# A scale block in two column halves, and a weight fold in three bursts, in a fused attention and feed-forward kernel

## The chip, the cores and the metric

The kernel runs on one core of a Trainium2 chip. The metric is the device time of one execution in microseconds (us). Engines go by the profile's short names: PE is TensorE's matmuls and PEld its weight loads, DVE is VectorE, ACT is ScalarE, POOL is GpSimd, SP is SyncE, which issues most DMAs.

## What is computed

A transformer block with adaptive layer norm. A conditioning vector `c` gives six modulation rows of 1024 (shift, scale and gate for each half of the block). The first half is a linear attention with 32 heads of 32, the second a SwiGLU feed-forward of width 3584. The sequence has 2048 rows.

```python
mod = (_silu(c) @ w_mod).reshape(c.shape[0], 6, 1, -1)
sa, ca, ga, sb, cb, gb = ...
h = _layernorm(x, axis=-1) * (1 + ca) + sa
x = x + ga * _A_ref(h, A_wqkv, A_wo)
h = _layernorm(x, axis=-1) * (1 + cb) + sb
x = x + gb * _B_ref(h, B_w_gate, B_w_up, B_w_down)
...
# _A_ref: qkv of x @ wqkv, phi(t) = where(t > 0, t + 1, exp(t)) + 1e-6
kv = jnp.einsum('bhsd,bhse->bhde', pk, v)
z = jnp.einsum('bhsd->bhd', pk)
num = jnp.einsum('bhqd,bhde->bhqe', pq, kv)
den = jnp.einsum('bhqd,bhd->bhq', pq, z)[..., None] + 1e-06
o = num / den
```

## The kernel before

The 2048 rows are worked in four super-tiles of 512 rows (`sc`), each of four row tiles of 128 (`t`). The 1024 columns of the model are eight blocks of 128 (`cc`, or `j` for the rows of `w_mod`). Weights and large activations live in a pool of 19 buffers of 8 KB per partition (`k8`, by `big`); input tiles and their normalised forms in `k2`; PSUM has two pools of four banks, `pa` (`acc_a`) and `pb` (`acc_b`). All matmuls go through `mm` (line 98), which keeps them on TensorE in the order of the program text, and transposes through `transpose` (line 101). In the opening, the block under `in_order` fixes the order of VectorE, ScalarE and GpSimd too. Elsewhere those engines are ordered by the compiler's scheduler, and `tc.issue_after` ties one instruction behind another on its engine.

The opening (lines 124 to 145 and 465 to 529) does this. SP loads two tiles of x, then the scale block of `w_mod` (`wca`, eight loads of 256 KB), then the value weights `wv` (eight loads) with two more x tiles among them, the shift block `wsa` (eight) and the key weights `wk` (eight). The conditioning vector is turned into a column tile `scT` with SiLU. Warming matmuls (`keep_warm`, `keep_warm_f32`) fill TensorE. `mod_rows(1, ...)` multiplies `scT`, spread over 32 columns (`sc32`), with the rows of the whole scale block, as row products into `mod_ps`; the first column block is also made as a column (`first`). `mod_turn` turns the rows by VectorE into columns `ca0T`. Meanwhile x tiles are normalised (`ln1_stats`, `ln1_norm`), transposed by TensorE (`pe_transpose_tile`) into `hT`, and scaled by `scale_to` into `hs`. The shift isn't needed for values at this point (it is added later through `vb`). Then come the value products `v_mms`: groups of a row tile and a column half, `k_groups`. Four groups (row tiles 0 and 1) run side by side through all eight `cc`, then the groups of tile 2, then of tile 3, with the shift block's rows between. At the end `modulate_all` makes the modulated `hT` in place for the key products (`k_phase`), which follow.

`sc_row`, the SiLU of `c` on every partition, is made by eight matmuls and two ScalarE copies (lines 485 to 489). It is used by `mod_step` on VectorE (line 396), which makes later modulation rows.

After the opening the phases are key, (`kv_phase` of the super-tile before,) value, and so on; then the query products (`q_phase`). The key-value product is folded into the output weights: `fold_wo` (lines 602 to 611) multiplies 32x32 blocks of `KVT` with rows of `wo`, and writes the result over `wo`. It is called four times, between query groups. Each call fills four banks of `pb`: for each of four column groups `i`, the four row groups `g`, 16 products in all. `wo_tile` uses the folded weights, and the feed-forward (`gate_up`, `down`) takes the rest of the time.

Of the kernel before, what the change touches and what calls it, by code (L numbers as in the profile page):

```python
# [8 lines left out]
ACT = mybir.ActivationFunctionType  # L9
# [12 lines left out]
def kernel(  # L22
# [91 lines left out]
    c_sb = const.tile([DC, P], BF16, name="c_sb")  # L114

# [8 lines left out]
    for st in range(2):  # L124
        load_x(st, nc.sync)
# [3 lines left out]
    wca = [big("wme", [4, D]) for _ in range(2)]  # L129
# [6 lines left out]
    for j in range(DC):  # L136
        load_block(wca, wm_v, j, D, nc.scalar if j == 0 else nc.sync)
    for cc in range(DC):
        load_block(wv, wqkv_v, cc, 2 * D)
        if cc in (1, 4):  # L140
            load_x(2 + cc // 4, nc.sync)
# [26 lines left out]
    sc_row = const.tile([P, D], BF16, name="sc_row")  # L168
# [35 lines left out]
    def normalise(dst, src, mean, rstd):  # L204
        nc.vector.tensor_scalar(out=dst, in0=src, scalar1=mean, scalar2=rstd, op0=ALU.subtract, op1=ALU.mult)

    def normalise_act(dst, src, mv, rstd):
        nmr = small.tile([P, 1], F32, name="nmr")
        last_nmr[0] = nc.gpsimd.tensor_scalar(out=nmr[:], in0=mv[:, 0, 0:1], scalar1=rstd[:, 0:1], scalar2=-1.0,  # L209
                                op0=ALU.mult, op1=ALU.mult)  # L210
        nc.scalar.activation(out=dst, in_=src, func=ACT.Identity, bias=nmr[:], scale=rstd[:, 0:1])  # L211
# [20 lines left out]
    def ln1_norm(sc, t, x_sb, mv, rstd, dve=False):  # L232
        xn = k2.tile([P, D], BF16, name="xn", bufs=4)
        if dve:
            normalise(xn[:], x_sb[:], mv[:, 0, 0:1], rstd[:, 0:1])
        else:
            normalise_act(xn[:], x_sb[:], mv, rstd)
        if sc > 0:
            last_load[0] = nc.sync.dma_start_transpose(hTs[sc][:, :, t * P:(t + 1) * P], xn[:])
        return xn  # L240
# [14 lines left out]
    def mod_rows(q, lo, hi, first=None):  # L255
        for j in range(lo, hi):
            if first is not None:
                mm(first, lhsT=wca[j // 4][:, j % 4, 0:P], rhs=scT[:, j:j + 1], start=False, stop=j == DC - 1)
            row_matvec(mod_ps[:, q * MW:(q + 1) * MW], sc32[:, j, :], (wsa, wca)[q][j // 4][:, j % 4, :],
                       q == 0 and j == 0, j == DC - 1)  # L260
# [195 lines left out]
    def keep_warm(acc, n):  # L456
        for _ in range(n):
            mm(acc[:], lhsT=sel[:, 0, :], rhs=sel[:], start=True, stop=True)

# [8 lines left out]
    keep_warm(spare, 1)  # L468
# [5 lines left out]
    with in_order(nc.vector, nc.scalar, nc.gpsimd):  # L474
        mod_ps = acc_b("mod_ps")
        mm(mod_ps[:, 0:DC], lhsT=c_sb[:], rhs=ident[0:DC, 0:DC], start=True, stop=True)
        for g in range(4):
            mm(mod_ps[g * DH:(g + 1) * DH, MW:2 * MW], lhsT=ident[:, 0:DH], rhs=base_t[:, 0:MW], start=True, stop=False)
        nc.scalar.activation(out=scT[:], in_=mod_ps[:, 0:DC], func=ACT.Silu)
        xn0 = ln1_norm(*ln1_stats(0, 0))  # L480
        st1 = ln1_stats(0, 1)
        nc.vector.tensor_copy(out=sc32[:], in_=scT[:].unsqueeze(2).to_broadcast([P, DC, DH]))
        xn1 = ln1_norm(*st1, dve=True)
        keep_warm_f32(spare, 1)
        for h in range(2):
            for j in range(DC // 2):
                mm(accs[h][:, j * P:(j + 1) * P], lhsT=scT[:, 4 * h + j:4 * h + j + 1].to_broadcast([P, P]), rhs=ident[:],
                   start=True, stop=True)
            nc.scalar.copy(out=sc_row[:, h * NB:(h + 1) * NB], in_=accs[h][:])
        keep_warm(spare, 3)  # L490
        first = accs[2][:, 0:1]
        mm(first, lhsT=ident[:], rhs=base_t[:, 0:1], start=True, stop=False)
        mod_rows(1, 0, 3, first)
        pe_transpose_tile(hT, xn0, 0)
        pe_transpose_tile(hT, xn1, 1)
        mod_rows(1, 3, DC, first)
        keep_warm(spare, 1)
        nc.vector.tensor_scalar(out=hs[:, 0, 0:H], in0=hT[:, 0, 0:H], scalar1=first, scalar2=None, op0=ALU.mult)
        mod_turn(DC, 2 * DC)
        for cc in range(1, 4):  # L500
            scale_to(hs, hT, cc, 0, H)
        xn2 = ln1_norm(*ln1_stats(0, 2))
        for cc in range(4, DC):
            scale_to(hs, hT, cc, 0, H)
        st3 = ln1_stats(0, 3)
        gs = k_groups[0:4]
        v_mms(hs, gs, accs, 0, 6)
        pe_transpose_tile(hT, xn2, 2)
        for cc in range(DC):
            scale_to(hs, hT, cc, H, H + P)  # L510
        xn3 = ln1_norm(*st3)
        v_mms(hs, gs, accs, 6, DC)
        gs2, accs2 = k_groups[4:6], [acc_b("acc") for _ in range(2)]
        v_mms(hs, gs2[0:1], accs2[0:1])
        v_evac(0, gs, accs)
        pe_transpose_tile(hT, xn3, 3)
        for cc in range(DC):
            scale_to(hs, hT, cc, H + P, SCW)
        v_mms(hs, gs2[1:2], accs2[1:2])
        mod_rows(0, 0, DC)  # L520
        mod_turn(0, DC)
        nc.vector.tensor_copy(out=sca[:], in_=scr[:, :, :, 0])
        v_evac(0, gs2, accs2)
        for g in k_groups[6:8]:
            acc = acc_a()
            v_mms(hs, [g], [acc])
            v_evac(0, [g], [acc])
        modulate_all(hT, ca1T, saT)
        nc.vector.tensor_copy(out=sc32[:], in_=saT.unsqueeze(2).to_broadcast([P, DC, DH]))
# [11 lines left out]
    for sc in range(NSC):  # L541
        if sc > 0:
            k_phase(sc, 0, 2)
            kv_phase(sc - 1)
            k_phase(sc, 2, 3)
# [40 lines left out]
        if sc == 0:  # L586
            with tc.issue_after(last_load[0].ins):
                last_load[0] = mod_load(2, gaT)

    q_phase(1, 0, 1, 2)  # L590
    q_phase(1, 1, 2)
# [10 lines left out]
    def fold_wo(h, nb):  # L602
        ns = slice(nb * NB, (nb + 1) * NB)
        ps = [acc_b("wf") for _ in range(4)]
        for i in range(HPC):
            for g in range(4):
                rs = slice(g * DH, (g + 1) * DH)
                mm(ps[g][i * DH:(i + 1) * DH, :], lhsT=KVT[rs, h, i * DH:(i + 1) * DH], rhs=wo[h][rs, i, ns],
                   start=True, stop=True)
        for g in range(4):  # L610
            (nc.scalar.copy if g % 2 == 0 else nc.vector.tensor_copy)(out=wo[h][:, g, ns], in_=ps[g][:])

    q_phase(1, 2, 5)
# [5 lines left out]
    den_sum(0, acc_a())  # L619
    fold_wo(0, 0)  # L620
    den_spread(0)
    q_phase(1, 6, 8)
    fold_wo(0, 1)
    q_phase(2, 0, 2)
    fold_wo(1, 0)
    q_phase(2, 2, 4)
    fold_wo(1, 1)
# [3 lines left out]
    def wo_tile(st):  # L631
# [10 lines left out]
        for nb in range(NNB):  # L642
            ns = slice(nb * NB, (nb + 1) * NB)
            a_ps = acc_b("a_ps")
            for hg in range(HG):
                mm(a_ps[:], lhsT=pq[:, hg, t * P:(t + 1) * P], rhs=wo[hg // 4][:, hg % 4, ns],
                                 start=(hg == 0), stop=(hg == HG - 1))
# [144 lines left out]
```

## Time and profile before

| What | Value |
|---|---|
| Median of 6 runs | 829.98 us (829.82 to 831.26) |
| Profiled execution, time | 830.38 us |
| Profiled execution, span from first to last instruction | 828.6 us |
| First value product starts | 11.80 us |
| First key product starts | 27.78 us |
| Four bursts of the fold start | 155.32, 159.24, 163.16, 167.09 us |
| x_sb loads: issue to landing, median | 5.3 us |

Times within the execution count from its first instruction. A line of a timeline has the start, the length, the engine, the line of the kernel, the operation and its output and inputs; "x16" means that 16 like instructions were merged, and a bracket says how long the engine was idle before and what ended that. A line of the chain of waits has a start, a length, and what the chain was on. The length of a single matmul contains its passage through the array, so successive ones overlap: the difference of two starts is what one costs.

### The profile page before, as it was taken

The numbers are of one execution on the slowest core, as the hardware profiler recorded it, in microseconds if no ns is written. First come the engines' busy times: TensorE is split into PE (matmuls) and PEld (weight loads), VectorE is DVE, ScalarE is ACT, GpSimd is POOL, SyncE is SP. The second block draws the span as 40 slices with busy tenths as digits, with TensorE's granted clock in tenths as the row PEclk, the third lists the DMA queues.
The fourth block names the chain that finished last, engine by engine and source line by source line (L and its number), as shares of the span: only waits on it lengthen the run. The fifth ranks groups of instructions, "written<-read, shape, count | busy, mean of one in ns | idle before, by whom it ended". The sixth has DMA issues, their size and how long they took to land.

```text
span 828.6 us, 11287 instructions
## 1 busy us (share of the span) xinstructions
PE 823.0 (99%) x4609; PEld 379.0 (46%) x4609; DVE 348.7 (42%) x680; ACT 168.3 (20%) x253; POOL 64.1 (8%) x165
## 2 busy tenths in 40 slices
PE   8999999999999999999999999999999999999998
PEld 4444444444444444444444444444444444444444
DVE  6868778886353344422222354222224432222222
ACT  3535343434111101101111010111111101111000
POOL 2101020120222101000000010000001100000000
PEclk9999999999999999999999999999999999999999
DMA  9978454139996736446242272753405529610011
GB/s 343 305 167 187 115 120 102 36 101 317 368 231 213 246 115 190 138 162 212 93 157 97 61 221 90 254 188 108 146 0 181 149 66 357 218 46 1 19 58 51
DMA packets 142212, 129.07 MB, mean 156 GB/s; under 512 B 58768, under 2 KB 120720, under 8 KB 141648
## 3 DMA queue, kind: packets, MB, share of 16 engines
q1 hardware_dynamic: 138208, 115.10, 46.2%
q0 software_dynamic: 3792, 12.98, 5.2%
q8 instruction: 36, 0.59, 0.3%
q10 hardware_dynamic: 160, 0.26, 0.1%
q14 instruction: 16, 0.13, 0.1%
HBM read 101.98 MB, written 12.72 MB: 138 GB/s over the span
## 4 chain that ended last, share of the span: by engine, by line
PE 98%; DMA 1%; DVE 0%; ACTq 0%; issue 0%
PE acc L98 90%; PE a_ps L98 7%; DMA wme<-in_w_mod_dram 1%; PE kvp L98 1%; PE wf L98 0%; PE den L98 0%; PE mod_ps L98 0%; PE tp L101 0%; PE vb L98 0%; ACTq L126 0%; DVE e L708 0%; DVE ob L711 0%
## 5 line engine op out<-in xcount | busy, mean ns | idle before, releaser
L98 PE MATMUL acc<-h2T,wgu 128*128 128x512 bf16 x1792 | 387.6, 379 | 0.0
L98 PEld LDWEIGHTS <-wgu 128*128 128x128 bf16 x1792 | 175.3, 98 | 211.3
L687 DVE TENSOR_TENSOR gu<-acc,e 128x512 bf16<-128x512 f32 x112 | 77.4, 691 | 289.9 <-PE acc L98 287.1
L98 PE MATMUL acc<-wd,gu 128*128 128x512 bf16 (+2 forms) x924 | 196.1, 373 | 0.0
L686 ACT ACTIVATE e<-acc 128x512 f32<-128x512 f32 x112 | 67.0, 598 | 374.7 <-PE acc L98 374.7
L98 PEld LDWEIGHTS <-gu 128*128 128x128 bf16 x924 | 89.3, 98 | 104.5
L708 DVE TENSOR_TENSOR e<-acc,gb_bc 128x512 f32<-128x512 f32 (+2 forms) x33 | 22.3, 675 | 131.7 <-PE acc L98 128.8
L98 PEld LDWEIGHTS <-hT 128*128 128x128 bf16 x448 | 43.6, 98 | 52.3
L98 PE MATMUL a_ps<-wo,pq 128*128 128x512 bf16 x256 | 57.4, 379 | 0.0
L98 PE MATMUL acc<-hT,wq 128*128 128x512 bf16 x256 | 56.7, 379 | 0.0
L98 PE MATMUL acc<-wk,hT 128*128 128x512 bf16 x256 | 56.4, 379 | 0.0
L273 ACT ACTIVATE eb<-acc 128x512 bf16<-128x512 f32 x64 | 37.7, 594 | 62.0 <-PE acc L98 59.8
L211 ACT ACTIVATE xn<-x,nmr,rstd 128x1024 bf16<-128x1024 f32 x16 | 19.8, 1240 | 126.2 <-POOL nmr L209 126.2
L98 PE MATMUL acc<-wv,hT 128*128 128x512 bf16 x192 | 41.9, 379 | 0.0
L98 PEld LDWEIGHTS <-pq 128*128 128x128 bf16 x256 | 25.1, 98 | 30.2
L655 POOL DMA_DIRECT2D x_scratch<-x x16 | 9.8, 615 | 373.4 <-DVE x L648 373.3
L98 PEld LDWEIGHTS <-wq 128*128 128x128 bf16 x256 | 24.6, 98 | 29.9 <-issue 1.1
L274 DVE TENSOR_SCALAR eb<-eb 128x512 bf16<-128x512 bf16 x64 | 18.3, 290 | 26.3 <-ACT eb L273 26.3
L648 DVE TENSOR_TENSOR x<-a_ps,x_sb 128x512 f32<-128x512 f32 x32 | 22.1, 691 | 8.6 <-PE a_ps L98 8.6
L195 POOL TENSOR_TENSOR rstd<-veps,neg_half 128x1 f32<-128x1 f32 x32 | 18.0, 562 | 99.6 <-DVE veps L193 86.8
L711 DVE TENSOR_TENSOR ob<-e,x1r 128x512 bf16<-128x512 f32 (+2 forms) x33 | 22.3, 675 | 1.0
L201 DVE BATCH_NORM_STATS2 stats<-x_sb 128x6 f32<-128x512 bf16 x32 | 20.9, 674 | 4.0 <-DMA x_sb<-in_A_x_dram 3.9
(99 smaller groups left out, 320.9 us busy)
## 6 DMA issues: line engine op xcount, KB each, us to landing
wgu<-in_B_w_gate_dram SPq DMA_DIRECT2D x28, 1024.0 KB, 7.0
wgu<-in_B_w_up_dram SPq DMA_DIRECT2D x28, 1024.0 KB, 8.1
x_sb<-in_A_x_dram SPq DMA_DIRECT2D x32, 256.0 KB, 5.3
x_scratch<-x POOLq DMA_DIRECT2D x16, 512.0 KB, 3.1
x1r<-x_scratch SPq DMA_DIRECT2D x31, 256.0 KB, 2.8
wd<-in_B_w_down_dram SPq DMA_DIRECT2D x7, 1024.0 KB, 7.3
rbc<-rden_scratch POOLq DMA_DIRECT2D x16, 256.0 KB, 8.5
out_dram<-ob SPq DMA_DIRECT2D x31, 128.0 KB, 1.7
```

The lines of the kernel that those rows point to most:

```text
L98: return tc.keep_in_program_order(nc.tensor.matmul(out, lhsT=lhsT, rhs=rhs, start=start, stop=stop))
L195: nc.gpsimd.tensor_tensor(out=rstd[:, 0:n], in0=veps[:, 0:n], in1=neg_half[:].to_broadcast([P, n]), op=ALU.pow)
L201: nc.vector.bn_stats(out=stats[:, i, :], in_=src[:, i * NB:(i + 1) * NB])
L211: nc.scalar.activation(out=dst, in_=src, func=ACT.Identity, bias=nmr[:], scale=rstd[:, 0:1])
L273: nc.scalar.activation(out=e[:], in_=acc, func=ACT.Exp)
L274: nc.vector.tensor_scalar(out=e[:], in0=e[:], scalar1=1.0, scalar2=PHI_EPS, op0=ALU.min, op1=ALU.add)
L648: nc.vector.tensor_tensor(out=x1[:, ns], in0=a_ps[:], in1=x_t[:, ns], op=ALU.add)
L655: nc.gpsimd.dma_start(out=x1_dram[st * P:(st + 1) * P, :], in_=x1[:])
L686: nc.scalar.activation(out=sg[:], in_=ps[0][:], func=ACT.Silu)
L687: gm = nc.vector.tensor_tensor(out=guT[sc][f // GPT][:, f % GPT, :], in0=ps[1][:], in1=sg[:], op=ALU.mult)
L708: nc.vector.tensor_tensor(out=yt, in0=y_ps, in1=gb_bc[:, ns], op=ALU.mult)
L711: nc.vector.tensor_tensor(out=ob, in0=yt, in1=x1r, op=ALU.add)
```

## The change

The scale block is loaded as two halves of 512 columns. The first half is computed as columns, each of four column blocks by 16 matmuls of one column into PSUM (`ca_cols`), beside the transposes, which are written to two PSUM tiles by column half (`turn_half`). VectorE scales the first half of row tiles 0 and 1 straight from PSUM by the PSUM columns; ScalarE makes the unscaled copies. The value products of row tiles 0 and 1 run over `cc` 0 to 3, then the second half of the scale block is made as rows (`ca_rows`), then row tile 2 runs over `cc` 0 to 3, and then all over `cc` 4 to 7. The first two tiles are both normalised by ScalarE, in two pieces. `sc_row` is now loaded as one row, put through SiLU on ScalarE, written to DRAM and loaded back on all partitions. The rows of the shift block stand between the two groups of row tile 3, and the last modulation runs in two row halves. `kv_phase` moves one key group forward, and one query group forward at the end. The fold writes to new tiles `wof`, and its 16 units run in three bursts of 5, 6 and 5.

```diff
-    for st in range(2):
+    for st in range(3):
         load_x(st, nc.sync)
...
-    for j in range(DC):
-        load_block(wca, wm_v, j, D, nc.scalar if j == 0 else nc.sync)
-    for cc in range(DC):
-        load_block(wv, wqkv_v, cc, 2 * D)
-        if cc in (1, 4):
-            load_x(2 + cc // 4, nc.sync)
+    def load_ca(h, eng0):
+        for k in range(4):
+            js = slice(2 * k, 2 * k + 2)
+            (eng0 if k == 0 else nc.sync).dma_start(out=wca[h][:, js, :], in_=wm_v[:, js, D + h * NB:D + (h + 1) * NB])
+
+    load_ca(0, nc.scalar)
+    nc.scalar.dma_start(out=sc_row[0:1, :], in_=c)
+    for cc in range(4):
+        load_block(wv, wqkv_v, cc, 2 * D)
+    load_ca(1, nc.sync)
+    load_x(3, nc.sync)
+    for cc in range(4, DC):
+        load_block(wv, wqkv_v, cc, 2 * D)
...
-        xn0 = ln1_norm(*ln1_stats(0, 0))
-        st1 = ln1_stats(0, 1)
+        xn0 = ln1_norm(*ln1_stats(0, 0), 2)
+        xn1 = ln1_norm(*ln1_stats(0, 1), 2)
+        st2 = ln1_stats(0, 2)
+        col0 = acc_b("col0")
+        cols = [col0[:, 0:1]] + [mod_ps[:, DC + i:DC + i + 1] for i in range(3)]
+        tps = [acc_b("tp", (4, H), BF16) for _ in range(2)]
+
+        def turn_half(xn, t, h):
+            for i in range(4):
+                transpose(tps[h][:, i, t * P:(t + 1) * P], xn[:, (4 * h + i) * P:(4 * h + i + 1) * P])
+
+        def ca_cols(k):
+            for i in range(4):
+                for j in (2 * k, 2 * k + 1):
+                    mm(cols[i], lhsT=wca[0][:, j, i * P:(i + 1) * P], rhs=scT[:, j:j + 1], start=False,
+                       stop=j == DC - 1 and i in (0, 3))
+
+        mm(cols[0], lhsT=ident[:], rhs=base_t[:, 0:1], start=True, stop=False)
+        mm(mod_ps[:, DC:DC + 3], lhsT=ident[:], rhs=base_t[:, 0:3], start=True, stop=False)
+        keep_warm_f32(spare, 2)
+        ca_cols(0)
+        turn_half(xn0, 0, 0)
+        ca_cols(1)
+        turn_half(xn0, 0, 1)
+        ca_cols(2)
+        turn_half(xn1, 1, 0)
+        ca_cols(3)
+        for cc in range(4):
+            nc.vector.tensor_scalar(out=hs[:, cc, 0:H], in0=tps[0][:, cc, :], scalar1=cols[cc], scalar2=None, op0=ALU.mult)
+        nc.scalar.copy(out=ca0T[:, 0:1], in_=cols[0])
+        nc.scalar.copy(out=ca0T[:, 1:4], in_=mod_ps[:, DC:DC + 3])
+        nc.scalar.copy(out=hT[:, 0:4, 0:H], in_=tps[0][:])
         nc.vector.tensor_copy(out=sc32[:], in_=scT[:].unsqueeze(2).to_broadcast([P, DC, DH]))
...
+        v_mms(hs, gs, accs, 0, 1)
+        turn_half(xn1, 1, 1)
+        xn2 = ln1_norm(*st2)
+        nc.scalar.copy(out=hT[:, 4:8, 0:H], in_=tps[1][:])
+        nc.scalar.activation(out=sc_row[0:1, :], in_=sc_row[0:1, :], func=ACT.Silu)
+        v_mms(hs, gs, accs, 1, 3)
+        pe_transpose_tile(hT, xn2, 2)
+        for cc in range(4):
+            scale_to(hs, hT, cc, H, H + P)
+        v_mms(hs, gs, accs, 3, 4)
+        ca_rows()
+        mod_turn(DC + 4, 2 * DC)
+        nc.vector.tensor_scalar_add(out=ca0T[:, 4:8], in0=ca0T[:, 4:8], scalar1=1.0)
         for cc in range(4, DC):
             scale_to(hs, hT, cc, 0, H)
+        gs2, accs2 = k_groups[4:6], [acc_b("acc") for _ in range(2)]
+        v_mms(hs, gs2, accs2, 0, 4)
+        for cc in range(4, DC):
             scale_to(hs, hT, cc, H, H + P)
+        xn3 = ln1_norm(*ln1_stats(0, 3))
+        v_mms(hs, gs, accs, 4, DC)
         v_evac(0, gs, accs)
+        v_mms(hs, gs2[0:1], accs2[0:1], 4, DC)
         pe_transpose_tile(hT, xn3, 3)
...
+        gs3, accs3 = k_groups[6:8], [acc_a() for _ in range(2)]
+        v_mms(hs, gs3[0:1], accs3[0:1])
+        mod_rows(lambda j: wsa[j // 4][:, j % 4, :], 0, DC)
         mod_turn(0, DC)
...
-            k_phase(sc, 0, 2)
+            k_phase(sc, 0, 1)
             kv_phase(sc - 1)
-            k_phase(sc, 2, 3)
+            k_phase(sc, 1, 3)
...
+            nc.gpsimd.dma_start(out=sc_dram[:], in_=sc_row[0:1, :])
+            with tc.issue_after(last_load[0].ins):
+                last_load[0] = nc.sync.dma_start(out=sc_row[:], in_=sc_dram[:].to_broadcast([P, D]))
...
+    wof = [big("wof", [4, D]) for _ in range(2)]
+    fold_units = [(h, nb, g) for h in range(2) for nb in range(NNB) for g in range(4)]
+
+    def fold_wo(accs):
+        units = [(fold_units.pop(0), acc) for acc in accs]
         for i in range(HPC):
-            for g in range(4):
+            for (h, nb, g), acc in units:
                 rs = slice(g * DH, (g + 1) * DH)
+                mm(acc[i * DH:(i + 1) * DH, :], lhsT=KVT[rs, h, i * DH:(i + 1) * DH],
+                   rhs=wo[h][rs, i, nb * NB:(nb + 1) * NB], start=True, stop=True)
+        for k, ((h, nb, g), acc) in enumerate(units):
+            (nc.scalar.copy if k % 2 == 0 else nc.vector.tensor_copy)(out=wof[h][:, g, nb * NB:(nb + 1) * NB], in_=acc[:])
...
+    den_sum(0)
+    fold_wo([acc_b("wf") for _ in range(3)] + [acc_a() for _ in range(2)])
     den_spread(0)
     q_phase(1, 6, 8)
+    q_phase(2, 0, 1)
+    fold_wo([acc_b("wf") for _ in range(4)] + [acc_a() for _ in range(2)])
+    q_phase(2, 1, 4)
+    fold_wo([acc_b("wf") for _ in range(4)] + [acc_a()])
```

## The prediction, before the changed kernel was run

> **What bounds the kernel now.** I read the page first: TensorE's share, and the chain that ended last.
>
> ```profile
> PE 823.0 (99%) x4609; PEld 379.0 (46%) x4609; DVE 348.7 (42%) x680; ACT 168.3 (20%) x253; POOL 64.1 (8%) x165
> ...
> PE 98%; DMA 1%; DVE 0%; ACTq 0%; issue 0%
> ```
>
> TensorE is the chain. What is not TensorE lies at the start, so I read the chain of waits in order of time next, at its two ends of interest: the opening and the fold of wo.
>
> ```profile
> 1.33 4.20 DMA wme<-in_w_mod_dram
> 5.53 0.02 issue
> 5.55 5.49 DMA wme<-in_w_mod_dram
> 11.04 0.05 issue
> 11.08 0.18 PE acc L98
> ...
> 155.39 0.36 PE wf L98 x16
> 155.75 3.56 PE acc L98 x16
> 159.31 0.36 PE wf L98 x16
> 159.68 3.56 PE acc L98 x16
> 163.24 0.36 PE wf L98 x16
> 163.60 3.56 PE acc L98 x16
> 167.16 0.36 PE wf L98 x16
> ```
>
> The loads of the scale block (wme, wca in the code) set the start until 11.04; from there TensorE never waits again. So two things count: when it begins dense work, and how much it is given. Then the timeline of TensorE at the start (start, length):
>
> ```profile
> 11.08 0.18 PE L98 MATMUL acc<-scT,wme 128*128 128x1 bf16 x1 [0.31 <-DMA wme<-in_w_mod_dram]
> 11.19 0.29 PE L98 MATMUL mod_ps<-wme,sc 128*32 128x256 bf16 x4
> 11.42 0.39 PE L98 MATMUL acc<-sel 128*128 128x512 bf16 x1
> 11.80 5.53 PE L98 MATMUL acc<-wv,hs 128*128 128x512 bf16 x24
> 17.16 0.61 PE L101 MATMUL tp<-ident,xn 128*128 128x128 bf16 x8
> 17.61 3.62 PE L98 MATMUL acc<-wv,hs 128*128 128x512 bf16 x16
> 21.06 0.61 PE L101 MATMUL tp<-ident,xn 128*128 128x128 bf16 x8
> 21.51 1.89 PE L98 MATMUL acc<-wv,hs 128*128 128x512 bf16 x8
> 23.33 1.06 PE L98 MATMUL mod_ps<-wme,sc 128*32 128x256 bf16 x32
> 24.32 3.63 PE L98 MATMUL acc<-wv,hs 128*128 128x512 bf16 x16
> 27.78 13.98 PE L98 MATMUL acc<-wk,hT 128*128 128x512 bf16 x64
> ```
>
> Last scale load in at 11.04, values at 11.80 (0.76 later: one column product, one DVE scaling of 0.29, the waits), keys at 27.78. And VectorE's timeline, for the load that follows the key weights:
>
> ```profile
> 29.07 1.88 DVE L201 BATCH_NORM_STATS2 stats<-x_sb 128x6 f32<-128x512 bf16 x3 [1.07 <-DMA x_sb<-in_A_x_dram]
> ```
>
> That x tile is the 37th load of 256 KB; the last scale load is the 10th. (29.07 - 11.04) / 27 = 0.667 us per load: the queue is full all through this stage, and any load's landing can be counted out.
>
> **What the Trainium skill says.** "TensorE: Matmul & The Clock Gate", Part 3 (The mechanism): small matmuls on different 32x32 tiles of the array run side by side, but matmuls start and end in strict program order. The trace agrees with the first half: 16 fold products take 0.36. The second half no run shows yet. "TensorEngine Tiling (Array Packing)", Key Properties: a change of tiling mode drains the array; the trace has it (below). The first page's Part 1: the array runs at half clock until it has been busy for about 3.4 us and falls back after as long an idle window. The trace agrees: float32 warming products start 0.43 apart up to 3.9 us and 0.22 apart at 5.14. "DMA: Bandwidth & Descriptors", Specifications: runs of 512 B and more go at line rate. The new loads have runs of 1 KB; the gate and up weights, with such runs too, moved 369 GB/s from 370 to 380 us, against 386 to 405 from 10 to 30. I take equal; the worst is 5%.
>
> **The opening, step by step.** The new order is x0 to x2, four loads of the first half block, four of wv, four of the second half, x3, wv's rest, shift block, wk. The first half is complete with load 7, three earlier: 11.04 - 3 x 0.667 = 9.04. Values begin at 9.04 + 0.76 + about 0.05 for the second row block of the column sum = 9.85. The rest is there: xn1's two ScalarE pieces (about 0.62 each, half of 1.24) follow the old nmr time 8.1 and end at 9.4; its first four transposes need the first piece alone. wv's first load is number 8, landing 9.7.
>
> Work of TensorE from values to keys, before: 27.78 - 11.80 = 15.98. After: 64 value products at 0.2165 (27.73/128 in the chain of waits) = 13.86, 0.16 at their start (5.36 less 24 x 0.2165); four transposes of xn1's second half, 0.225 (half of a tile's 0.45); two tiles, 0.90; the second scale half as rows, which moves behind the start of values: 32 products of 128 columns. Nearest row: the denominator's 32 products of the same width, 0.56; with 0.09 for the switch, 0.65 (ends 0.5 and 1.0, the last being the 256-column rows' price). The shift rows, 0.99 + 0.09. Sum 16.88, so 0.90 more than before; keys at 26.73 if nothing waits.
>
> Waits on the way. Second half: load 15, at 14.37; its rows begin about 13.9, run as the loads come and end at about 14.75, no later than without the wait. Its turn, add and scaling on DVE (about 0.28, 0.15, 4 x 0.22) hide behind eight value products (1.73). xn2 must pass ScalarE behind the small copies and a 1024-wide copy of about 1.1: ready at 12.5, wanted at 12.6. x3: DVE reaches its statistics at 17.0, POOL has nmr by 19.7, ScalarE xn3 by 20.95; its transposes are wanted at 20.8: 0.2. Its scaled copy then costs another 0.15. The last wv load lands at 17.7 (wanted 19.1), the last shift load at 23.0 (24.2). Keys at about 27.1. The last wk load, number 36, lands at 28.4; the first key group wants it 1.5 after its start: met, but keys can't gain much more than this. Modulation in halves gives its first column 0.8 before it is wanted. Gain 0.7; ends 0 (xn2 and xn3 each half a microsecond later) and 1.1.
>
> **The fold.** Before: the last query product before a burst starts 158.93, the first fold product 159.24, the next query 159.61. Beyond the query's own 0.2165 a burst costs 0.464 (3.93 - 16 x 0.2165 gives the same). Four: 1.855. In it the i loop is outside and the four row groups inside: 16 products, 16 different tiles. After, the same 64 products in bursts of 5, 6 and 5 units. Within one i the fifth unit meets the row group of the first, and with the same i the same tile. It must wait until that one has streamed its 512 columns (about 0.213, the query's time without its 3 ns), and in program order all later products wait behind it. The next i can start beside the late unit, so a burst takes five rounds, not one: 0.464 + 4 x 0.213 = 1.316. Three: 3.95. Cost +2.1. If free tiles may overtake, two rounds: 3 x 0.677 = 2.03, cost +0.2. I take 2.1 as program order is what the skill states.
>
> **At nothing.** Separate wof tiles: two more buffers alive only during the fold, when wv, v3 and pk3 are free; later wo goes where it stayed before. Six evacuations a burst (0.59 on ScalarE, 0.68 on DVE, three each) finish 2.4 after it, before the second next query group wants its bank. kv one key group earlier: the last v copy is done a microsecond before. sc_row by a write, a broadcast load and a DMA on POOL, ahead of the transposed loads on SP's queue (45.66 before): all idle then, first use at 63.6; uncovered, about 2. Its silu on ScalarE (1.2) sits ahead of nothing urgent before xn3. Fewer warming products: see the rival.
>
> **Sum.** -0.7 + 2.1 = +1.4. On the profiled execution, 830.38 (span 828.6 and 1.8 around it), 831.8; on the runs' median 829.98, 831.4. The profiled one is 0.4 above the median, which I take off.
>
> **Rivals.** (a) Forecast: rounds in the fold, opening gains 0.7: 831.4. 0.57. (b) The fold hardly pays (free tiles overtake): 829.98 - 0.7 + 0.2 = 829.5. For it: 16 starts lie within 0.05, so starts are cheap; against: the same tile can't stream two operands, and order is strict. 0.18. (c) Slower: a cold array at the values. The old order kept it busy to 4.36 and warmed it about 5.0; the new one drops a bf16 product there and three before the rows, and column products are short. If the window that ends near 8.4 isn't busy enough, values start at half clock until 11.8: 2 us at half work, 1.0 lost, up to 1.7 for a whole window; with (a) 832.4 to 833.1. It decides if value products begin over 0.3 apart. Against: transposes and column products fill most of 6 to 9. 0.20. (d) Faster beyond measurement: the fold as in (b) and the opening worth 1.7, if x and half block come faster than counted: 828.1. The wk landing at 28.4 stands against it. 0.05.
>
> **Chances.** A measurement here tells about 0.2%, 1.66 us: below 828.3 or above 831.6. (a) spreads about 0.7 around 831.4: 0.38 of it is slower, some of it through order in the schedule that I can't see: 0.22; (c) all slower. Slower 0.42; faster (d) and a part of (b), 0.10; same 0.48. Range 829.2 to 833.0: from (b) through (c).
>
> **What would show it.** First value product at 9.85, first key product near 27.1; fold groups in three bursts of about 1.2 from first fold to next query product. Wrong: bursts of 0.6 (b); values 0.43 apart (c); a wait before the transposes of xn2 or xn3 over 0.5; any TensorE wait after the keys.

## The result, and the profile after

| | Before | Changed |
|---|---|---|
| Median | 830.10 us (829.42 to 831.26, 32 runs) | 832.54 us (831.00 to 833.33, 14 runs) |
| Profiled execution: time, span | 830.38, 828.6 | 831.24, 829.4 |
| First value product | 11.80 | 9.67 |
| First key product | 27.78 | 28.37 |
| Fold bursts, first fold product to next query product | 0.37 (four of them) | 0.59, 0.60, 0.58 |

The ratio of the times is 1.0026, with a 95% interval of 1.0019 to 1.0033: slower by about 2.2 us. The forecast of 831.4 is 1.1 below the median, which lies inside its range. The sum came out near the truth; two of its terms did not, as the profile shows at once. The page first, TensorE's share and the chain:

```profile
PE 823.2 (99%) x4619; PEld 379.3 (46%) x4619; DVE 346.9 (42%) x685; ACT 172.5 (21%) x260; POOL 65.0 (8%) x167
...
PE 98%; DVE 1%; DMA 0%; POOL 0%; ACT 0%; issue 0%
```

TensorE is still the chain. The DMA share of the chain, 1% before, is gone: the start no longer hangs on the scale loads. TensorE's timeline shows what became of that:

```profile
8.78 0.40 PE L101 MATMUL tp<-ident,xn 128*128 128x128 bf16 x4 [0.33 <-ACT xn L219]
9.01 0.19 PE L98 MATMUL col<-scT,wme 128*128 128x1 bf16 x2
...
9.67 1.89 PE L98 MATMUL acc<-wv,hs 128*128 128x512 bf16 x4 [0.31 <-DVE hs L506]
11.35 0.63 PE L101 MATMUL tp<-ident,xn 128*128 128x128 bf16 x4
...
23.81 1.90 PE L98 MATMUL acc<-wv,hs 128*128 128x512 bf16 x8 [0.21 <-DVE hs L271]
...
28.37 13.98 PE L98 MATMUL acc<-wk,hT 128*128 128x512 bf16 x64
```

Values start 2.13 earlier than before. But the first four take (11.35 - 9.67) / 4 = 0.42 each, not 0.2165, and the keys start 0.59 later. The windows of that stretch (busy time of PE, PEld, DVE, ACT, POOL, then the granted clock PEclk, the DMA share and GB/s) give the reason:

```profile
8.00:9.00 1.00, 0.67 (x16) 0.58 (x15) 0.43 (x3) 1.00 (x2) 0.42 (x1) 1.00 1.05 405
9.00:10.00 1.00, 0.69 (x13) 0.41 (x11) 0.74 (x3) 0.59 (x2) 0.46 (x3) 0.57 1.06 406
...
11.00:12.00 1.00, 1.00 (x7) 0.65 (x6) 0.00 (x0) 1.00 (x2) 0.00 (x0) 0.50 1.08 357
...
13.00:14.00 1.00, 1.00 (x7) 0.50 (x6) 0.00 (x0) 1.00 (x2) 0.00 (x0) 1.00 1.06 378
```

TensorE is busy for 0.67 of the time just before the values, with short transposes and column products. From 9.1 to 12.5 the clock is 0.5: the trace's record of the clock, which begins at 5.72, has 1.0 for 3.413 us, 0.5 for 3.413 us, and 1.0 from then on. In the kernel before the clock is 1.00 in all these windows, and TensorE is busier in the first of them:

```profile
8.00:9.00 1.00, 1.00 (x19) 0.86 (x20) 0.42 (x2) 0.38 (x1) 0.00 (x0) 1.00 1.05 401
```

In the fold, TensorE's timeline of the first burst has (wf and acc are banks of the two PSUM pools):

```profile
156.12 0.39 PE L98 MATMUL wf<-wo,kvs 32*32 32x512 bf16 x3
...
156.18 0.59 PE L98 MATMUL acc<-wo,kvs 32*32 32x512 bf16 x5
156.71 0.39 PE L98 MATMUL acc<-hT,wq 128*128 128x512 bf16 x1
```

The last group holds one product that starts at 156.18 and four later ones. A narrower window, which has those four alone:

```profile
156.35 0.42 PE L98 MATMUL acc<-wo,kvs 32*32 32x512 bf16 x4
```

So 16 products on 16 different tiles start within 0.06. The four of the fifth unit, each on the tile of the first unit with the same `i`, start from 156.35 to 156.40, each 0.23 after the one whose tile it takes. In the program each of these four stands directly behind its own group of four, ahead of the groups of the next `i`. They have been overtaken, and not by a new order of the program: the 20 weight loads of the burst still come in fives, and from one group of four to the next the starts leave a gap for the missing one, 6 to 7 ns (10 ns in the burst of six units), where it is 3 to 4 ns within a group and in all 16 of a burst before. A burst is two rounds long, not five. The span's +0.8 in these two executions is the keys' 0.6 and the fold's 0.2; it leaves open why the median rose by 2.4.

### The profile page after: what moved, and what is told of

It is laid out like the page before. It is cut to its first block, busy times and chain, and to the rows that moved or that the text cites. A ratio compares the mean times of both kernels' runs of the same rounds, so it can differ in the third digit from the quotient of the medians.

```text
span 829.4 us, 11326 instructions
## 1 busy us (share of the span) xinstructions
PE 823.2 (99%) x4619; PEld 379.3 (46%) x4619; DVE 346.9 (42%) x685; ACT 172.5 (21%) x260; POOL 65.0 (8%) x167
## 4 chain that ended last, share of the span: by engine, by line
PE 98%; DVE 1%; DMA 0%; POOL 0%; ACT 0%; issue 0%
PE acc L98 90%; PE a_ps L98 7%; PE kvp L98 1%; DMA x_sb<-in_A_x_dram 0%; DVE stats L209 0%; PE tp L101 0%; PE den L98 0%; PE mod_ps L98 0%; PE wf L98 0%; PE vb L98 0%; ACT xn L219 0%; DVE hT L229 0%; POOL rstd L203 0%; DVE mv L210 0%; DVE hs L506 0%
## 5 line engine op out<-in xcount | busy, mean ns | idle before, releaser
L98 PE MATMUL a_ps<-wof,pq 128*128 128x512 bf16 x256 | 57.4, 379 | 0.0
L219 ACT ACTIVATE xn<-x_sb,nmr,rstd 128x1024 bf16<-128x1024 bf16 (+1 forms) x18 | 20.3, 1143 | 19.0 <-POOL nmr L214 18.9
```

Source lines behind the costliest of these rows:

```text
L98: return tc.keep_in_program_order(nc.tensor.matmul(out, lhsT=lhsT, rhs=rhs, start=start, stop=stop))
L219: nc.scalar.activation(out=dst[:, ws], in_=src[:, ws], func=ACT.Identity, bias=nmr[:], scale=rstd[:, 0:1])
```

## Experiments

Each kernel ran beside the kernel before on the same chip; medians of before were 830.02 (first four runs below), 829.96 (e5 to e8), 829.94 (e9 to e11) and 830.00 (e12).

| Run | What it is | Median (range), runs | Ratio to before, 95% |
|---|---|---|---|
| e2 | before + new fold | 830.26 (829.83 to 831.17), 13 | 1.0001 (0.9993 to 1.0009) |
| e3 | changed, old fold | 831.85 (831.05 to 833.17), 9 | 1.0023 (1.0013 to 1.0032) |
| e4 | before, less warming | 832.09 (829.68 to 833.26), 22 | 1.0021 (1.0014 to 1.0028) |
| e1 | changed, more warming | 832.50 (831.25 to 833.06), 9 | 1.0027 (1.0018 to 1.0036) |
| e5 | e1, gate block ahead of x | 830.70 (830.16 to 832.24), 21 | 1.0011 (1.0004 to 1.0017) |
| e6 | changed, gate block ahead of x | 835.00 (833.62 to 836.69), 5 | 1.0063 (1.0051 to 1.0076) |
| e7 | e1, modulation whole | 832.79 (832.04 to 833.63), 5 | 1.0037 (1.0023 to 1.0051) |
| e8 | before, late modulation | 830.39 (829.64 to 831.68), 13 | 1.0007 (0.9999 to 1.0015) |
| e9 | changed, gate block behind wq | 831.76 (830.85 to 832.92), 16 | 1.0021 (1.0014 to 1.0029) |
| e10 | e1, gate block behind wq | 830.56 (830.18 to 832.12), 13 | 1.0008 (1.0000 to 1.0017) |
| e11 | e10, old fold | 830.81 (829.83 to 832.01), 21 | 1.0012 (1.0005 to 1.0019) |
| e12 | changed, again | 831.78 (831.05 to 833.59), 11 | 1.0024 (1.0015 to 1.0033) |

### The fold alone, and taken out: e2, e3

e2 puts the new `fold_wo`, its three calls and `wof` into the kernel before; e3 puts the old ones back into the changed kernel.

```diff
-    fold_wo(0, 0)
+    fold_wo([acc_b("wf") for _ in range(3)] + [acc_a() for _ in range(2)])
...
-    fold_wo(0, 1)
-    q_phase(2, 0, 2)
-    fold_wo(1, 0)
-    q_phase(2, 2, 4)
-    fold_wo(1, 1)
+    q_phase(2, 0, 1)
+    fold_wo([acc_b("wf") for _ in range(4)] + [acc_a() for _ in range(2)])
+    q_phase(2, 1, 4)
+    fold_wo([acc_b("wf") for _ in range(4)] + [acc_a()])
```

> The kernel before with the new fold alone: tiles of its own, bursts of 5, 6 and 5 units. Theory free tiles overtake: bursts of about 0.59 from first fold product to next query product, 2.06 in all against 1.855, time +0.2 over before, 829.9 to 830.7. Rival strict program order: bursts of about 1.2, time +2.1.

> The changed kernel with the old fold (four bursts, written over wo). Theory cold array plus overtaking fold: -0.2 against the changed kernel, about 832.3, with the same spread of runs (831 to 833). Rival that the fold or its extra buffers cost most of the 2.4: near 830.

The new fold alone costs 0.2 at the median (830.26 against 830.02, an interval of -0.6 to +0.7), and its bursts last 0.58, 0.60 and 0.59. The 2.1 that the forecast charged is excluded. Without the new fold the changed kernel is still 1.8 above before, so the loss lies in the opening or what it moves. The profile of e3 has two things to show for it: its clock record has 0.5 for 6.827 us, two windows, with keys at 29.41; and a wait of 1.07, nine products behind the first kv phase, put down to issue:

```profile
63.28 2.97 PE L98 MATMUL acc<-wk,hT 128*128 128x512 bf16 x13 [1.07 <-issue]
```

### The cold array: e4, e1

e4 takes from the kernel before all its warming products but the three float32 calls at the start, and leaves all else. That is a little more than the change takes: it drops the five bf16 products, but has one float32 call more than before.

```diff
     keep_warm_f32(spare, 3)
-    keep_warm(spare, 1)
...
-        keep_warm_f32(spare, 1)
...
-        keep_warm(spare, 3)
...
-        keep_warm(spare, 1)
```

> The kernel before without its warming products, but for the three float32 ones at the very start. Theory cold array: TensorE's share in the window before the values falls as in the changed kernel, the first value products start 0.42 apart in all or some runs, time +1 to +2.5 with a wide spread. Rival (warming doesn't matter there, the row products keep the array busy): time within 0.3 of before.

The profiled execution, TensorE's timeline:

```profile
11.85 7.01 PE L98 MATMUL acc<-wv,hs 128*128 128x512 bf16 x24
...
29.32 1.89 PE L98 MATMUL acc<-wk,hT 128*128 128x512 bf16 x8
```

The 24 products that took 5.53 before take 7.01, and keys come 1.5 later; the record has 0.5 for 6.827 us. A window of 3.413 at half clock takes 0.002 from the mean clock over the span, which is kept for each run. It sorts many of the 22: three with 1.000 took 829.68 to 829.75, three with 0.998 (one window) 830.39 to 830.64, six with 0.996 (two windows) 831.96 to 832.35. One window costs 0.8, two cost 2.4. It does not sort all: two more with 1.000 took 830.53 and 830.96, and eight 832.74 to 833.26. The clock record of a profile begins some microseconds into the execution, so an array that first becomes warm later would leave no half in the mean; that is a guess. A mean clock of 1.000 is therefore no proof that an array was warm.

e1 adds seven products of 512 columns to the column stage of the changed kernel, whose results are not used.

```diff
         ca_cols(0)
+        keep_warm(spare, 3)
         turn_half(xn0, 0, 0)
         ca_cols(1)
+        keep_warm(spare, 1)
         turn_half(xn0, 0, 1)
         ca_cols(2)
+        keep_warm(spare, 2)
         turn_half(xn1, 1, 0)
         ca_cols(3)
+        keep_warm(spare, 1)
```

> The changed kernel with seven bf16 warming products (zero operands, result unused) put into TensorE's waits between the column products of the opening. Theory cold array (the window from about 5.0 to 8.5 us isn't busy enough, so the array runs the first values at half clock for at least one window of 3.4 us): the first value products start 0.22 apart instead of 0.42, the keys start near 27.1 to 27.3 instead of 28.37, and the time falls to about 829.3 to 830.2, and its runs lie within 0.5 of one another where the changed kernel's spread over 2.3. Rival order of work (the opening is late because ScalarE and VectorE are late with xn2, xn3 and the scaled copies): the values still wait, keys near 28, time 831 to 832.5.

The mean clock is 1.000 in all nine runs, and in the profile the values are no later and 0.22 apart. Keys come at 27.22, 1.15 earlier than in the changed kernel. But the median does not move (832.50 against 832.54). TensorE's timeline, in the opening and about the first kv phase:

```profile
9.64 1.04 PE L98 MATMUL acc<-wv,hs 128*128 128x512 bf16 x4
...
29.15 2.10 PE L98 MATMUL acc<-wk,hT 128*128 128x512 bf16 x9 [0.26 <-DMA wk<-in_A_wqkv_dram]
...
57.08 1.22 PE L98 MATMUL kvp<-v,pk 128*32 128x64 bf16 x128
58.24 0.60 PE L98 MATMUL acc<-wk,hT 128*128 128x512 bf16 x2
60.43 5.77 PE L98 MATMUL acc<-wk,hT 128*128 128x512 bf16 x26 [1.59 <-issue]
```

The gain is given back in two waits. 0.26 is for a key weight block, the limit that the forecast had seen. 1.59 is for nothing that the profile names: TensorE stands still two products behind the 128 small products of the kv phase.

### What "issue" is: e5 to e11

The queue of instruction packets (queue 8 in the page's DMA part) moves 36 packets of 16 KB, and TensorE has 4619 matmuls and 4619 weight loads, so a packet holds some 256 of its instructions. The kv phase uses up a packet's worth in 1.15 us. My theory from e1 and e3: the packet due there is late, because it goes over the DMA engines, and these are full of the transposed gate-block loads (`mod_load(2)`). SP issues those later in the changed kernel. The gate block is two such loads; the groups of four below hold these two and the two of a later block. SP's issues before and changed (start, length of the group):

```profile
45.66 26.48 SPq L380 DMA_TRANSPOSE wmt<-in_w_mod_dram  x4
```

```profile
49.69 23.02 SPq L385 DMA_TRANSPOSE wmt<-in_w_mod_dram  x4
```

The group's line gives the start of its first load alone. In the trace the second load of the gate block leaves at 50.84 before and 56.92 changed, and lands 1.8 ahead of the first kv product before and 7.7 behind it changed. The loads stand behind the transposes of the next `hT`, the x loads and the new `sc_row` reload. In the changed kernel the modulation of `hT` takes VectorE 4.19 in 16 pieces (2.67 in 8 before) and the next tile's statistics start at 31.75, not 29.07. The rival: the wait comes from the new order of work itself, not from DMA.

e6 (changed) and e5 (e1) put the gate block ahead of the reload and of the x loads:

```diff
-        if sc + 2 < NSC:
-            for st in range((sc + 2) * STC, (sc + 3) * STC):
-                with tc.issue_after(last_load[0].ins):
-                    load_x(st, nc.sync)
         if sc == 0:
+            with tc.issue_after(last_load[0].ins):
+                last_load[0] = mod_load(2, gaT)
             nc.gpsimd.dma_start(out=sc_dram[:], in_=sc_row[0:1, :])
...
-            with tc.issue_after(last_load[0].ins):
-                last_load[0] = mod_load(2, gaT)
+        if sc + 2 < NSC:
+            for st in range((sc + 2) * STC, (sc + 3) * STC):
+                with tc.issue_after(last_load[0].ins):
+                    load_x(st, nc.sync)
```

> The warmed kernel of the first round with the transposed loads of the gate block (wmt) issued ahead of the sc_row reload and of the next x loads instead of behind them. Theory fetch behind loads: TensorE's instruction block, read over the same DMA engines, comes late because the transposed loads, issued at 48.75 us there (45.66 before), still run while the first kv phase uses up a whole block in 1.2 us; issued about 2.5 earlier, they end before the fetch, the wait put down to issue after that phase (1.6) goes, and the time falls from 832.5 to about 829.8 to 830.8, with a narrower spread. Rival (the fetch is late for another reason, such as the kv phase one key group earlier): the wait stays, 832 to 832.7.

> The changed kernel, not warmed, with the same reordering of the loads. Theory two losses, cold array and late fetch: only the fetch part goes, 830.8 to 831.8, and its runs still spread by what the cold windows cost (about 1 to 1.7). Rival cold array alone: no change, 832.5. Rival fetch alone: as low as the warmed one.

The same edit helps one and harms the other. e5 is 1.8 faster than e1, and has no wait behind the first kv phase. e6, forecast near 831, is 2.5 slower than the changed kernel. Its TensorE timeline and SP's issues:

```profile
59.31 1.22 PE L98 MATMUL kvp<-v,pk 128*32 128x64 bf16 x128
...
64.90 2.32 PE L98 MATMUL acc<-wk,hT 128*128 128x512 bf16 x10 [2.31 <-issue]
```

```profile
48.59 8.93 SPq L385 DMA_TRANSPOSE wmt<-in_w_mod_dram  x2
...
58.24 1.80 SPq L123 DMA_DIRECT2D x_sb<-in_A_x_dram  x4
```

The first gate load left 1.1 earlier than in the changed kernel and the second 3.9 earlier (53.01), landing 0.2 behind the first kv product; but the x loads now fell on the kv phase. It also ran cold through two windows (keys at 29.80). So an earlier place in the queue is no cure by itself: the edit put other loads where the transposed ones had been.

e7 gives e1 the undivided modulation, and e8 gives the kernel before the late shift rows and the modulation in 16 pieces:

```diff
-        for lo in (0, H):
-            for cc in range(DC):
-                modulate(hT, cc, ca1T, saT, lo, lo + H)
+        modulate_all(hT, ca1T, saT)
```

```diff
         v_mms(hs, gs2[1:2], accs2[1:2])
+        v_evac(0, gs2, accs2)
+        gs3, accs3 = k_groups[6:8], [acc_a() for _ in range(2)]
+        v_mms(hs, gs3[0:1], accs3[0:1])
         mod_rows(0, 0, DC)
...
+        v_mms(hs, gs3[1:2], accs3[1:2])
+        v_evac(0, gs3, accs3)
+        for lo in (0, H):
+            for cc in range(DC):
+                modulate(hT, cc, ca1T, saT, lo, lo + H)
```

> The warmed kernel with the first modulation in eight whole instructions instead of sixteen halves. Theory: VectorE is free 1.5 us earlier (2.67 against 4.19), the next statistics, transposes and so the transposed gate loads start 1 to 2 us earlier, part of the wait goes: 830.5 to 832. Rival that VectorE's lateness has nothing to do with it: 832.5.

> The kernel before with the shift rows between the last two value groups and the modulation in sixteen halves, as in the change, and nothing else of it. Theory fetch behind loads: the keys start at 27.8 as before, but the next statistics come 2 to 3 us later and with them the transposed loads; TensorE shows a wait of 0.5 to 2 put down to issue after the first kv phase, time 830.5 to 832. Rival: no wait after the keys, 830.0 to 830.3.

Both missed. In e7 the first gate load leaves at 45.81, as early as before, and the wait is still there (0.94 at 60.16). But the second leaves at 54.32, only 2.1 earlier than in e1 and 3.5 later than before, and lands 4.7 behind the first kv product: the edit did not take the loads out of the way. In e8 they leave at 47.82 and 52.94, 2.2 and 2.1 later than before, the second lands 2.6 behind the first kv product, and there is no wait. So their time of issue alone does not decide.

e9 (changed) and e10 (e1) move the gate block right behind the loads of `wq`, where it lands over 10 us ahead of the kv phase; e11 is e10 with the old fold.

```diff
         with tc.issue_after(last_load[0].ins):
-            nc.sync.dma_start(out=wq[h][:], in_=wqkv_v[:, 4 * h:4 * h + 4, 0:D])
+            wq_load = nc.sync.dma_start(out=wq[h][:], in_=wqkv_v[:, 4 * h:4 * h + 4, 0:D])
+    with tc.issue_after(wq_load.ins):
+        last_load[0] = mod_load(2, gaT)
...
-            with tc.issue_after(last_load[0].ins):
-                last_load[0] = mod_load(2, gaT)
```

> The changed kernel, not warmed, with the transposed gate loads issued right behind the query weights (about 28 us) instead of at 49.7. Theory fetch behind loads: the loads are over long before the first kv phase, the instruction fetch there is served at once, no wait put down to issue of over 0.3 between 55 and 67 us; what is left is the opening with its cold windows and the fold's 0.2: 830.8 to 831.8, with a spread of about 1.5 from the cold windows. Rival (the fetch is late without these loads too): 832.5 or more.

> The same with the seven warming products. Both losses taken away: keys at 27.2, no wait after the first kv phase, 829.5 to 830.2 with a spread under 1. Against the unwarmed one it gives the price of the cold array by itself, 0.8 to 1.7. Rival (cold array costs nothing in the end, as the first round's warmed kernel was no faster): no difference between the two.

> The same, warmed and with early gate loads, and the old fold in four bursts. Theory: 0.2 less than with the new fold, 829.3 to 830.0, that is even with the kernel before or a little faster. If the new fold cost more than its bursts show, more than 0.5 less.

e10 is 1.9 faster than e1. e10 and e11 stay above their forecasts, by 0.4 and 0.8. The window of 58 to 60 us, e1's first and then e10's (columns as above, in a window of 2 us):

```profile
58.00:60.00 2.00, 0.84 (x39) 0.40 (x26) 1.32 (x4) 0.00 (x0) 0.00 (x0) 1.00 0.98 108
```

```profile
58.00:60.00 2.00, 1.84 (x10) 0.93 (x11) 1.05 (x3) 0.12 (x1) 0.00 (x0) 1.00 0.03 8
```

e1's window begins 0.9 behind its first kv product, e10's 1.2. A DMA share of 0.98 goes with a PE busy for 0.84 of 2.00, and a share of 0.03 with 1.84. TensorE's timeline of e10:

```profile
56.78 1.22 PE L98 MATMUL kvp<-v,pk 128*32 128x64 bf16 x128
58.16 9.01 PE L98 MATMUL acc<-wk,hT 128*128 128x512 bf16 x41 [0.16 <-issue]
...
116.56 12.03 PE L98 MATMUL acc<-wk,hT 128*128 128x512 bf16 x54 [0.79 <-issue]
```

The 0.16 is one matmul whose record is missing from the trace. The wait of the first kv phase is gone. Behind the third, at 116.56, a shorter one remains, 0.4 to 0.8 in e1, e5, e10 and e11. No kernel without the seven warming products has it.

What "issue" stands for can be counted out. In e1, e3, e6 and e7 TensorE stops with the same number of instructions done, 479 weight loads and 478 products (by the loads where records of matmuls are missing). That is not the same place of the program: two products behind the kv phase in e1 and e7, nine in e3 and e6, seven fewer with the seven warming products. The waits behind the third phase come after 990 weight loads, 511 pairs later: 1022 instructions, with two semaphore instructions between them 1024, which is four packets of 256. So TensorE stops where a packet ends, and the place moves through the program with the number of instructions ahead of it.

In the table "place" is the number of products between the kv phase and that count of 479 loads, "starts" the start of the due packet, counted from the first kv product of the same execution, and "lead" the time from this start to the last of the 479 loads:

| Profile | Place | Packet starts | Lead | Wait behind the kv phase |
|---|---|---|---|---|
| before, e2, e8 | 11 | -1.33, -0.90, +0.25 | 4.65, 4.22, 3.08 | none |
| e4 | 18 | -0.85 | 5.69 | none |
| changed, e12, e9 | 9 | +0.31, +0.39, +0.33 | 2.58, 2.51, 2.56 | none |
| e10, e11, e5 | 2 | -1.46, -1.46, -1.07 | 2.84, 2.84, 2.46 | none |
| e3 | 9 | +1.55 | 1.34 | 1.07 |
| e7 | 2 | +0.22 | 1.16 | 0.94 |
| e1 | 2 | +0.63 | 0.76 | 1.59 |
| e6 | 9 | +3.19 | -0.30 | 2.31 |

A lead of 2.46 or more goes with no wait, one of 1.34 or less with a wait, and in the four with a wait TensorE resumes 2.4 to 2.8 after the packet's start. The later waits of e1, e5, e10 and e11 fit: there the lead is 1.4 to 1.8. This explains e8 too: its packet is 1.2 later than e2's, but the old order has 11 products to do until it is needed.

That the wait is a late packet is thus shown. The order of work is not the cause: with the same order on TensorE, e1 has the wait and e10 has not. Why the packet is late is shown in part. In e1, e3 and e7 a gate load is in flight when it starts, and against e10's (for e1 and e7) and e9's (for e3) it is late by 2.1, 1.7 and 1.2; the edits that take these loads away or move them ahead, e10 and e5, take the first wait and 1.8 to 1.9 of the time away. But the changed kernel and e12 also have a gate load in flight, with the DMA engines as full, and their packets start when e9's does. So such traffic can delay the packet and need not. Why e6's is late by 2.9, when the gate loads had landed and only x loads and the `sc_row` reload ran, stays open.

### The changed kernel again: e12

> The changed kernel once more, unedited, because its one profile so far shows no wait behind the first kv phase while two kernels equal to it up to that point nearly so (the fold undone: 1.07) show one. Theory of the late fetch: the wait is there in some executions and not in others, by whether the transposed gate-block loads meet the fetch; this profile has a wait of 0.5 to 1.6 put to issue between 58 and 65 us, values 0.42 apart, and a time of 832.0 to 833.2; if it has none, the time of this profiled run is below 831.6. Rival: the wait belongs to the edited kernels alone and the spread of the changed kernel is only the cold window; then no such wait, and a run above 832 has two windows at half clock (two times 3.4 us).

Its profiled execution took 831.21, has one half window (values 0.42 apart, keys at 28.48) and no wait. So neither profile of the changed kernel itself shows the late packet; e3, the same up to the fold, does. For the changed kernel the case rests on times. Its 25 runs have a mean of 832.21, and the 16 of e9 831.69: 0.5 more, with a standard error of 0.2. At equal clock the gap is alike: 832.3 against 831.9 (medians, mean clock 1.000, 3 and 5 runs), 831.5 against 831.1 (0.997 to 0.999, 12 and 7 runs) and 833.0 against 832.3 (0.995 and 0.996, 10 and 4 runs). These are from different jobs, so the 0.5 is less firm than the rest.

## Why the prediction was right, and where it was wrong

**Start of values: the time was right, the reason was not.** 9.85 was forecast, 9.67 measured, and the scale block in halves takes the scale loads off the chain. But the forecast had the last half load, at 9.04, set the start. In the trace the third half load lands at 7.69, 0.7 ahead of the count, and what comes last is the second tile's normalised form: its transposes wait 0.33 for ScalarE at 8.78, and the last column products follow them at 9.01 without a wait. That the two ways give nearly the same time is luck.

**The fold: wrong.** The step that failed is "in program order all later products wait behind it". Bursts take 0.6, not 1.2 or 1.3; +2.1 was charged and the runs show +0.2 (e2), the number of rival (b). The Trainium skill, "TensorE: Matmul & The Clock Gate", Part 3 (The mechanism), has matmuls start in program order; the measurement decides otherwise here, for products on free 32x32 tiles.

**The cold array: rival (c), given 0.20, is what happened.** Value products 0.42 apart were its sign. It priced one window at 1.0 and up to 1.7; the changed kernel ran at half clock for one window in some executions and two in others, and the difference of e9 and e10, which are both clear of the late packet behind the first kv phase, is 1.2. That is a net figure: e10's profile pays 0.79 behind the third phase, which e9's does not, so the cold array may have cost up to 2.0 (an estimate, the sum of the two). "Against: transposes and column products fill most of 6 to 9" was the wrong judgement: 0.67 of the time in short products did not hold the clock. All 14 profiles agree on this. In the first window of 3.413 us of each clock record, all at 1.0, TensorE is busy for 0.53 to 0.70 in the six whose clock then falls (e4, e3, e6, changed, e12, e9, in this order), and for 0.75 to 1.00 in the eight that keep it (e5 lowest, then before and e1 with 0.79). Whether the share decides or the kind of product was not separated: the warming products are long ones. Part 1 of the same page (The HAM clock gate) gives the window as about 3.4 us, running freely so that its place differs from run to run. The record agrees with the length (3.413), and the change from one half window to two between executions fits the second.

**The opening's gain of 0.7, even warm: wrong in two terms.** From values to keys the forecast was 17.25 (16.88 and 0.35 of waits); e10 has 17.57, e1 17.58. There TensorE waits (from the starts, at 0.2165 a product) 0.26 ahead of the third tile's transposes, 0.20 ahead of the fourth's and 0.36 behind those. And the base was a late one: in e2 and e8, whose opening up to the values is that of the kernel before, values start at 10.86 and 11.06 and keys at 27.02 and 26.92, not 11.80 and 27.78. Against those, a warm new opening (keys at 27.18 in e10) gains nothing. But the profiled executions of e2 and e8 are the fastest of their 13 runs each, as the one of before is 0.3 above its median, so the usual start lies between. By the times, e10 less 0.8 for its late wait and 0.2 for the fold is 0.4 below before: the gain of a warm opening is between nothing and 0.4 (an estimate). The forecast took off 0.4 for this execution's lateness but still took the opening's gain from it.

**Loads with runs of 1 KB: no loss is shown.** They were taken as equal, with 5% at worst. The DMA summary of 10 to 15 us, changed and before:

```profile
DMA packets 1528, 1.87 MB, mean 373 GB/s; under 512 B 115, under 2 KB 1119, under 8 KB 1528
```

```profile
DMA packets 1100, 2.03 MB, mean 405 GB/s; under 512 B 118, under 2 KB 118, under 8 KB 1099
```

That is 8% less in these 5 us. But from 5 to 10 us the changed kernel moved more (384 against 363 GB/s), and from 5 to 20 both moved 5.8 MB. By the single packet, the changed kernel's trace from 10 to 15 us has 46 ns for 1024 bytes and 84 ns for 2048 (medians), 10% more per byte. "DMA: Bandwidth & Descriptors", Specifications, puts the line rate at 512 bytes and above; these packets do not agree. Whether e1's 0.26 for `wk` comes of it is not shown.

**Costed at nothing: sc_row, the divided modulation and the moved kv phase.** Each has cover for itself. Together they push SP's queue back by 4 to 6, and so the transposed loads onto an instruction packet; how much each pushes was not separated. "Any TensorE wait after the keys" stood among the signs of error, but no step looked at how the engine gets its instructions. 0.5 in the changed kernel, 1.9 in the warmed one (e1 less e10).

**The sum.** The changed kernel's 25 runs have a median of 832.27, 2.2 above before. The runs split it into about 0.5 for the late packet (changed less e9), 0.2 for the fold (e2), and some 1.5 for the opening, which is the cold array less what the earlier start gains. e10, with the array warm, is still 0.6 above before; its profile has the 0.79 behind the third kv phase, which comes with the seven warming products, and the fold's 0.2 (e10 and e11 do not differ measurably). The forecast had +2.1 for the fold and -0.7 for the opening. Its total was near by luck: an overcharged fold stood in for an array that it took to be warm, and for a late packet that it did not know of. No version beat the kernel before; e2 and e10 equal it within their intervals or nearly.

## What to carry to other kernels

When small products take the place of row products ahead of dense work, look at TensorE's busy share in the windows before that work: here a start 2.1 earlier on a cold array brought the next stage 0.6 later, and the cost varied from run to run, so one profile understated it. Where hundreds of short matmuls follow one another, keep the DMA engines free of heavy loads just before, and when a wait is put to issue, count the engine's instructions up to it: stops at equal counts in different programs point to a late packet of instructions. A few products more or less ahead of such a place move it, as the seven warming products did. And before a gain is taken from when loads land in one execution, ask how much that moves between executions of the same code: here 0.7 to 0.9, as much as the gain.

## What the runs showed of the hardware that was not expected

- Products on free 32x32 tiles overtook an earlier one that waited for its tile: 16 starts within 0.06, and four others, which stand between them in the program, each 0.23 after the one whose tile it takes.
- TensorE's instructions come in packets of 16 KB over the DMA engines. With transposed loads in flight the packet came 1.2 to 2.1 late in three kernels, and TensorE stood for 0.9 to 1.6 behind 128 small products, always after 479 weight loads. A packet that started 2.46 or more ahead of that place cost nothing.
- The clock fell to half for whole windows of 3.413 us, one or two, after a window at full clock with TensorE busy for 0.53 to 0.70; after 0.75 or more it stayed full. With seven more products of 512 columns the mean clock was 1.000 in all nine runs of e1.
- Packets of 1 KB took 46 ns and packets of 2 KB 84 ns at the median, 10% more per byte; over 15 us the bytes moved were the same.
